# Sparse attention and a gated feed-forward block on one core: the same work under another static table of order and engines

## The chip, the cores and the metric

One core of one Trainium2 chip. The metric is the device time of one launch in microseconds, a median over runs. The engines are PE (TensorE, with its weight loads as PEld), DVE (VectorE), ACT (ScalarE), POOL (GpSimd) and SP (SyncE, which here only issues transfers). All of them work through their own instruction lists in order.

## What is computed

```python
scores = scale * np.matmul(q, k.transpose(0, 1, 3, 2))    # 8 x 8 heads, 576 x 576, depth 64
mask_local = (rel >= 0) & (rel < 32)                       # heads 0 to 3
mask_strided = (rel >= 0) & (pos[None] % 32 == pos[:, None] % 32)   # heads 4 to 7
attn = softmax(np.where(masks, scores, -1e9))
x = np.matmul(attn, v)                                     # to 4608 tokens x 512
xn = x / rms(x) * rms_g
out = (silu(xn @ w_gate) * (xn @ w_val)) @ w_out           # 512 -> 1536 -> 512
```

All in float32; the three weights come as 64-bit-wide arrays and are made into float32 on the chip.

## The kernel before, in words

**Products.** [...] Each product is then three PE products: high by high, weight low by high, high by low. A group of three on 512 columns is called a *triple* here; it is one planned operation (lines 565, 641, 1194, 1417; line 1618 has two of them). The gate and value products of chunks 0 to 2 are plain; those of the later chunks, and the output products of all but chunk 0, go in pairs of chunks by a scheme that saves one in eight products of half size (Strassen's).

**Attention.** The 64 heads are done two at a time: 32 visits. For visit n there are the scores Sn (line 291: 72 or 80 small matmuls into the bank pair, each counted as one record of 64 columns), the softmax (mask L311, maximum L314, ten exponentials on ACT L318, reciprocal L322 and L323, scaling L325, transposition L327), the values Vn (line 303) and the evacuation into a buffer raw (L361 on ACT or L363 on DVE). S0 to S4 and V0 to V3 come first and make chunk 0 of the tokens (512 of 4608); the rest is spread among the products of the feed-forward block. Visits 5 to 7 have their values in two halves.

**Chunk 0.** Each of its four quarters of x is made into xh and xl (L528 or L532, L539), squared (L400 on POOL, L403 on ACT) and summed over the partitions by PE (L408). DVE makes the root from the sums (from L485), PE spreads it (L496, the *spread*), ACT copies it (L499) and DVE multiplies the first gate products by it (L575). g(u) and v(u) stand for the gate and value products of 128 columns of the weights, each of four triples, one for each quarter of x.

**Weights.** For each block SP fetches 512 KB (L1746, names wg, wv, or), ACT makes two steps (L1761, L1766), DVE two (L1771, L1776), ACT the high part (L1781), and DVE or POOL the low part (L1783); SP writes most of them back to memory for later use (L1787, L1790). A load of q or k (L265, 288 KB) needs the slot that earlier scores read, a load of v (L275, 384 KB) the slot that earlier values read.

**Warm-ups.** Two products of ones by zeros into the bank v (L230) have no reader; they stand first on PE.

**Order.** No operation is issued as it is planned. Each is entered in a list with what it reads and writes; the constant ORDER, compressed, then gives the whole list in another sequence and for each operation the engine that takes it (many can be done by DVE or POOL, others by ACT or DVE). Within an engine the sequence is the order of its instructions. Dependencies become semaphore waits; nothing else holds an engine back, except that its instructions must have been fetched: PE's code comes in pieces of its own through the same 16 DMA engines as the data.

```python
        code = zlib.decompress(base64.b85decode(ORDER))
        left, out = list(range(n)), []
        for k in range(n):
            i = left.pop(code[k] + 256 * code[n + k])
            out.append(self.ops[i][0][ENGINES[code[2 * n + k]]][2])
        return out
```

Of the kernel before, what the change touches and what calls it, by code (L numbers as in the profile page):

```python
# [56 lines left out]

ENGINES = ("PE", "DVE", "ACT", "Pool", "SP")
ORDER = (
    "c-rk)*^^zxdGD{gPxsmPyYJiFduQJ?qir-|MrZ>hKp+VaMjMih%pyn>NyeC+f)oJ<0|5hN8yo@U;8X=WB#z@aen{mZ52?Jze?VSbsr&)y(|yjJG0%BP)ttFA_e`JeZ~c"  # L60
# [3 lines left out]
    "2%1g2wh&UYh(tTz{|o+;eUxddBtMdiuhtu6xaWwb+VZF2pZCdG3Yy)T_^WufFoYD~m6^wCKHXs`6sB@Vs~Ro>S%T+@R06*RJ2?N7wcrS$XQol`GM;+v?ZW{`l%4KYD8K"
    "l`B!<`kw9+{^Mcp$|IAH=C)5<+V$}A!{>LN>)!v(%V(+`|KifJe!g{voQY=U9=zh6dVJPfyf0Y)W-vc>Y463Ucu#O9+Iz>;>V-@DiVv(e&jp1u!>D&G9}Ox;kGEQtdyY"
    "+Z8^>x#@2aCF1cz_y)(;gAm-jdKSNFquxMQF5tHP>QDD5d&I}1DK^V{dD%{Vu;yIh;C<(6~RiaD&t{dl2OrW2)b*eVW&gX&n(ndwe<bNPv4J~s&CX~&5>PB(heZ9fq{{"
    "&*{Nzts*K)v#6xz0%q0nQHKzpnRiHDg^iCPnPn<pb#C)htcKY_P`E{yBE)v!ufp#&z}k7x!Aci8jnhDvFy8EvE{k$zOuXK7RjpT1iM|wbGMJ{jhD9#8Vg`~vsG`p;`N;"
    "!<E8Oo*($Z?dL_FxRV-ezD?{7Pjg8$A+uf+(w)P7_jrLlz;Rar<x@x;+ce!LY%k^TZTB?-FPNC@7`C)$dAU|QpWAVMs{zCJv_FV2rJm09#PBm@UcB*UD1Lv#zs;gtBCA"
    "75~J4-v9qEoOc1v_UKV(Uz9VA<y%WL99VnT|`0V|Hkk1JgJ2p4oNH_CC|JEz=CxZo^%f<&JLi<we~b8b*KG2&W9O5bA@5Zue}jrCF^KYuwOTt#Xy+b^2rsG>o630U=$#"
    "L&iMPv`O72(<YfTCWtj8Cq;Gl?`2~l30vKe_S(ch&>pMTYBldjwd#GlS~)}y&XO52P1Z<>jPD^G(r=UVwAmpIjm(p(cvz`SHKxe;1R=u#>65`2VZHSpS?;i%VYHo)`pR"  # L70
    "s5M&x6ColKGn*#m>!U;^}@``<9r{yj|nMw^7ja1z5fhC!tcJ?D!t=yaQ(wJQy1)XOy}PgP(s_b(6+R`VM4!tVGA{Mm3<=e5Bi{m%vPUYzR<nz%pqAB~&ijh}QUdw9G#b"
    "a5Y`Rfcj2suzouH_CrMSuR(gR4VqMaH>=KVt5mF41g|OWzk*T5<E5cc!fSXgD>aT>wYf(=ee?9_D}n}iaQT1`iljBzV+>xOgB6T8o?f@joDQ=-^rIDZx$f7at}g$Du@C"
    "IrcQ{&z_Fo!7wdZrtgfxKtcyTR!vo#XcVlKU&=!tqSc~TlJsVFs6O++_;kcs@Rs!q~EzCM?XPN1(CGOf)yuiXU6Ksezo#IM|1f`%}4Ct--X8z8`tv*z|;_gbmO7=Ga+Z"
    "R_BcrYJ_md<@+ezH96OyjUofFRcjT34HvW(H=BA2z@_pi|Ba7J%j-^8oLm?C#m+kM6V~T!h;KjIho)S=9zw=X|Tv(^r~aXWJs-bIx&K6`RZ<6OS8ssKZ~6?dQRl``~l0"
    "o4?t}vwGh<#d?CV;r-w3E^5|0Lg|ub&c9*c*L73pZipz;Ug)@*)7EVC56FgV2K~jH0XhtL#6y$!B8Lr4OE-+0bwmGgGt_xb*FNy`?*X&5z}9^&%(<=>IGSVstD`&o-za"
    ";Qg(hK|RwmRY_Rq<e)C?cd1I8{8&2esyopChXA||2aBrocmAQndq=K`Fg2Xi#S<Tcy3iTkWYY9=v?*Gu*dqn;;E5rTgaYB&$%a{R?31Vza5!L-1zEU4aJgdahnDDqj2H"
    "TYf#Z^QwK-xT%qI&q2rqT~EkNUR?5tY?UUv4stWHO>ez5dxiGd{e)`UvJZM;51CY@R|Xjy>cHtsZqc>2Eg<>J&dlRf5r$9N0$&mUlIEp`Vw6L<2*-aJ%+G-lU7miF+vO"
    ">jhdVyqQ67mCZcyEz848q1W^sa5>9r2_=k&|2?V<a+kq`1WM8Lv$|To4f+x^n`_V(@l_KpKYpvBLvhP_T=*-U3cmY*jpA)hQh2rGjtrsvFFcS`H1iW4ZxE<gDc&HZaE-"
    "#t>lE1AqE4EHPG~*g?<n+d1s?ezS{d{=D-`>!xO~HUQYep|2o;Uf9!c3npa~>=hA@cO8hY;^~#x+ATPWVT(yjMYWw|ba|i=|so%Z_L4>9HJ}sIuIGxvkHN0gKqwLdd+j"
    ">+?0&CF`yB{2z6-*_Fq9%UkYRv|gdc#YJj9T+r!ciTAAuJD-m&-oBkMQuE!Gqpz32=cbE{$Ux@yvxqw|w}YWsYhkH^4D3%9g~vLJY-VB8#YWj~QmaVsna?9*CjUH(bo3"  # L80
    "1FGd#6_(#EJ@0g87$7TXnA4mtR!a?V4)#ivEw1tU0G-_}Hh;U@18y^?2TPPLfkv|Fi2j^X)B9^Pp>DB!xu9m6(gPUkx3U0{qjHWk<~fER3^yAd``xa`{G2@4=E00XBnE"
    "dWdsEZ}5tXo$Dt4lxtP)hURx2GfCKk75lI{Cy_QaG;t-Ii<Yc6BamR&=LT(#qU+q;zZX-UZ@0*xdM;`&bnaPV46bONw7h)Oij}`*EHME-~iS1HNK`%&7@T0z}jSqX~f`"
    "^Q4ksdMErmPP*<oDR&nYwQA<EQE_CoG0El=XtOaw9&j!~FgFoGK_4Zg491V|fe%L$QjLz{3Vtia(JF{v-@xlB~Fjqd*9N77fx<R+?=ks`$b*70R9+<_vPp}QUI+Q^(r;"
    "%F3CLt(65rFj^R`0TE9|biHp)z7clrN$ZDxzbE=g^6x_z?2<&F!O}wN4MLI@HjFf?I@FtBkh95q2k=JGg(FJ-d$PZ_%dLHRIq4?hkZ;=(!$j)1XD6al6}_frHSo%U4jT"
    "G%TThab;*08V`<@+S^NJeS5L8e7tzv%-vba&6v05hG=|X9PCHc-BAvOQE#ak1$DjeM^#h__o3!s(q&FA=O9}!5t;L<xa=a|nDuhYMsLYogxh%s^txy2mZOKd=`#b0+IB"
    "7yQFVzn0}N>sh+5RdHpjfyE^u1TF<RCTA$yB?5{pEH0v9fh9WM|W^O?iAW?7oXxXZz|!4`0H1H(6nt2>wz+|YEbY6v#)nK&SRLP6)ABk0V;y2!l^goqUmUY9Y)F$D-s0"
    "Z4~_=Gd&zx0o3-AvM9afUOuyEXKs1384lAQZXX}`?Q2H<==&;O)z3%VQ}r5=6OGJ!KaVH7s$*ZgbWK^K#^@AavJD6Cyu|51PfA~VZnfRX$T{F`|S}uOrO!H#pxcpYGAG"
    "*VIU$4XaU%T`O8E@GX}PFQK1Ow2*v0DqkG?p6G%ULuZ>X6LKOpD#;ZIk@D*bp$7@VK&XylSM?}hfM3G^%33{Tb;h{P3ygk(D8Yen-V@JcDJ82LQq13c#q{sD3z&paElD"
    "8KcK|81g)o%o~5-iRDpxkV2`tniJHF1o6J+~I(Mu0utUeQmiT6)vkg(@hXqcc`GA6rwF=#j=P<Ay_hMqN$EyXL80oiR)L(v&erG*R99L`4tuzD|32hr~9kSY=`s%)A&e"
    "BU`fs&v4QBL}Ro?pE9NA=_RTb2{X5@t!wMry0)&ZYwOy&wyyv07i@)K>)N`uuKyc0!Gx0J0swJ?l3PkBrQ#zo1&YNBgV-hRL9F0pCHWBx;sGEmzg_|?K5vQ@D)-9mn5M"  # L90
    "@e*^;c2<eB^<woo8g3PB{<hmr$ASfU~kBy}Sx5+z@NA+c3FBFV@5M1G=Jya-n6ki6SiS1-JIfuwhIbVMo`Jr&xMf9R(3G`&krOZF3WoQyPoO(DrdD@jTdN$wE-+AH-i*"
    "?=<-WEfM)QadOEGC}f<$RkNSWOUMBVIcXs=PJ}>v)W9XG%^c6lEQ$bCM3a^?#m}KH_2|YVYw6!N`y#>IswwK)YU8**`Z9L@<^<vo5T-EoskcTT9iJi93`TOvLw|bPi7`"
    "00>x>n#E$j~u~Y#g*+Q^1GzD0q5Q%6d;FZ>j%~D`y2vzx$qH$_v<{i!~$TZ35A^BxXvQAU@66F^j`IDeoW-xOIh>97>oJc_@UswfSnUHCh9*crR$q|_(>6WsBDBDM|B$"
    "@D3#V9E>!ve*dvqDleD07%*fB{tr3adofN?;V7R02u?lQ4&pAlFC|NU9<Y8zrjjkX0w|1oR{~5VTQ6$pVrUhag2UR_T#$66uNDtpY<--X)?^IAHm27CP7z;EboFKnxpj"
    "OfX1sx+_Uh7F2nwXhwkwsfejcBq@CnB|R}$g_B4;NN**hAyqU~WpD$-Nt_dt6oyoEQou_Nl#0{JO@WQm$D4VJWQ)RtWM2xv%@jmaE|dg7Q&y3g%$PS#CQUK2ndwpsh%!"
    "kyO-As;lH;*LM~0@fM*iTQX0GFGQ5Itw6Por9EHkZ?5~UiGj7?~o7E#T316N79Wgyj`B$u-KB~=n7LLo#l4VIj?(VCK{BrzZfahiKcJc@fIzYxVVQk(LCq*%a;N+_iHO"
    "?fhTmJ~(emnt(=LR7U+8SoUB((1(N6ppfODq2!d$MPsn3Q8HSfGy9FL^a8}w2F!Bm!L>V;uEVvB9cZ(x`U((AP*|-*%_4zmG87XvnG_arIh2cPLWkwiX5u^qpB8Exe=6"
    "31j>J`T6<bdIE8<5lNNc_Qxp<2Wio!FdP;$*sxj?QIO`xd?Tu*}%M#mE^2&mA9-vCr2>6?Dn>r<F38Rf-g0vN=>X+{rZS)SD8l{*w?ao-COO+fRDV6~y3h2qZ#F)(3$k"
    "DVgA#Im(J>gN6>oh=#k7`^)3T<f(OBu2iq7ks90=bgf0(4UhA=|H{Wwn+nPDi#BmM{uzqDP?zA;ntRNjlmn#>|wPQ-Z>ZtBH&U%Al4yO0#K@$P^Mqb}0$S4w603fSHYj"
# [1825 lines left out]
```

## Time and profile before

| | |
|---|---|
| median of 3 runs | 925.74 us (924.26 to 926.48) |
| profiled execution | 925.52 us, span 923.5 us |
| PE, PEld, DVE, ACT, POOL busy | 98%, 80%, 80%, 51%, 27% |
| PE matmuls | 8722 |
| instruction queue of PE's code (q8) | 69 packets, 1.13 MB |
| data moved | 220.78 MB, mean 239 GB/s |

Times in rows are microseconds from the start of the span. A row of a timeline merges neighbours of one form: start, length, engine, line, operation, tiles, count, and in brackets the idle time before it with what ended it. "issue" in a chain or a bracket is time in which the engine waited for nothing that the profile shows. [...]

### The profile page before, as it was taken

What the parts mean: (1) busy time and instruction counts of PE and PEld (TensorE: products, weight loads), DVE (VectorE), ACT (ScalarE), POOL (GpSimd) and SP (SyncE); (2) the same over time, 40 slices, a digit from 0 to 9 for tenths busy, and PEclk for the clock granted to TensorE, in tenths of its full rate; (3) what the DMA queues carried; (4) which work ended last, traced back from release to release, by engine and by line L of the source; (5) the groups of instructions that cost most, each with busy time, mean ns of one, the idle gap of its engine ahead of it and who ended that gap; (6) DMA issues with size and microseconds to landing.
All of it is one profiled execution on the core that took longest, in us unless ns stands there. A gap on an engine that the chain in (4) does not pass through costs nothing.

```text
span 923.5 us, 21815 instructions
## 1 busy us (share of the span) xinstructions
PE 903.0 (98%) x8722; PEld 735.0 (80%) x8722; DVE 739.2 (80%) x1219; ACT 469.4 (51%) x1324; POOL 249.8 (27%) x216
## 2 busy tenths in 40 slices
...
GB/s 314 261 348 257 173 337 235 253 276 299 151 219 193 309 255 295 380 126 246 296 190 166 233 244 362 291 161 238 191 167 184 243 337 221 178 229 250 184 169 103
DMA packets 95093, 220.78 MB, mean 239 GB/s; under 512 B 9616, under 2 KB 28688, under 8 KB 94992
## 3 DMA queue, kind: packets, MB, share of 16 engines
...
q8 instruction: 69, 1.13, 0.5%
...
HBM read 172.17 MB, written 47.19 MB: 238 GB/s over the span
## 4 chain that ended last, share of the span: by engine, by line
PE 96%; DMA 1%; issue 1%; DVE 1%; ACT 0%; SPq 0%; DVEq 0%
PE acc L1618 11%; PE acc L1417 8%; PE acc L565 8%; PE v L1618 7%; PE g L1618 7%; PE v L565 7%; PE g L565 7%; PE v L1417 5%; PE g L1417 5%; PE acc L641 4%; PE g L1029 4%; PE v L1029 4%; PE acc L1029 4%; PE pair L291 3%; PE pair L303 3%; PE v L1194 2%
## 5 line engine op out<-in xcount | busy, mean ns | idle before, releaser
L565 PE MATMUL g<-xh,wg 128*128 128x512 f32 x184 | 59.3, 404 | 0.0
L565 PE MATMUL v<-xh,wv 128*128 128x512 f32 x184 | 58.3, 398 | 0.0
L318 ACT ACTIVATE pp<-pp,mx 128x64 f32<-128x64 f32 x160 | 53.3, 339 | 6.7 <-DVE mx L314 6.7
L318 ACT ACTIVATE pT<-pT,mx 128x64 f32<-128x64 f32 x160 | 53.4, 340 | 6.3 <-DVE mx L314 6.2
L696 POOL TENSOR_TENSOR tt<-tt 128x256 f32<-128x256 f32 (+1 forms) x32 | 27.5, 866 | 71.0 <-DVE tt L696 49.7
L291 PEld LDWEIGHTS pair<-xx,xx 64*32 64x32 f32 (+1 forms) x2432 | 27.8, 109 | 22.1 <-issue 14.8
L291 PE MATMUL pair<-xx,xx 64*32 64x64 f32 (+1 forms) x2432 | 33.9, 234 | 10.3 <-issue 5.3
L565 PEld LDWEIGHTS g<-xh,wg 128*128 128x128 f32 x184 | 34.9, 194 | 7.4 <-issue 0.2
L565 PEld LDWEIGHTS v<-xh,wv 128*128 128x128 f32 x184 | 33.5, 188 | 7.2 <-issue 0.2
L565 PE MATMUL g<-xl,wg 128*128 128x512 f32 x92 | 36.7, 399 | 0.0
L361 ACT COPY raw<-pair 128x160 f32<-128x160 f32 (+8 forms) x61 | 20.2, 376 | 31.3 <-PE pair L303 31.2
L565 PE MATMUL v<-xl,wv 128*128 128x512 f32 x92 | 35.9, 390 | 0.0
L565 PE MATMUL acc<-xh,wg 128*128 128x512 f32 x104 | 34.2, 411 | 0.0
L565 PE MATMUL acc<-xh,wv 128*128 128x512 f32 x104 | 33.0, 398 | 0.0
L1636 ACT ACTIVATE or<-g 128x512 f32<-128x512 f32 x24 | 14.3, 597 | 33.2 <-PE g L1618 32.2
L318 ACT ACTIVATION_READ_ACCUMULATOR pT<-pT,mx 128x1 f32 x160 | 30.9, 193 | 0.0
L318 ACT ACTIVATION_READ_ACCUMULATOR pp<-pp,mx 128x1 f32 x160 | 30.7, 192 | 0.0
L641 PE MATMUL acc<-or,hh 128*128 128x512 f32 x96 | 30.0, 394 | 0.0
L1618 PE MATMUL acc<-wg,wv 128*128 128x512 f32 x102 | 28.6, 389 | 0.0
L1618 PE MATMUL acc<-wv,wv 128*128 128x512 f32 x102 | 28.6, 389 | 0.0
L303 PEld LDWEIGHTS pair<-pT,vt 32*64 32x64 f32 x784 | 17.9, 136 | 9.1 <-issue 5.6
L303 PEld LDWEIGHTS pair<-pp,vt 32*64 32x64 f32 x744 | 17.8, 140 | 8.4 <-issue 4.0
...
## 6 DMA issues: line engine op xcount, KB each, us to landing
wv<-wsv SPq DMA_DIRECT2D x36, 512.0 KB, 7.0
wg<-wsg SPq DMA_DIRECT2D x26, 512.0 KB, 6.8
or<-tg SPq DMA_DIRECT2D x22, 512.0 KB, 5.8
tl<-tg SPq DMA_DIRECT2D x21, 512.0 KB, 5.7
th<-tg SPq DMA_DIRECT2D x21, 512.0 KB, 5.0
...
```

Of the source, the lines that this page charges most:

```text
L291: nc.tensor.matmul(out=pair_[32 * y:32 * y + m, h, 64 * g:64 * g + 64], lhsT=q[r, PAD + a:PAD + a + m], rhs=k[r, a:a + 64], start=True, st ...
L303: nc.tensor.matmul(out=dst[z // 2][64 * h:64 * h + 64, z % 2, 320 + c:320 + f], lhsT=v[r, 6 * h + j], rhs=t[r, a:a + f - c], start=j == fi ...
L318: nc.scalar.activation(out=tv[:, g], in_=tv[:, g], func=AF.Exp, bias=m[:, g:g + 1], accum_out=z[:, g:g + 1])
L361: nc.scalar.copy(out=d, in_=s)
L565: nc.tensor.matmul(out=out, lhsT=wt[:, w, sl], rhs=xhl[x, kc], start=(n == 0 and i == 0), stop=(n == KC - 1 and i == 2))
L641: nc.tensor.matmul(out=acc[t], lhsT=x[h][:, sl], rhs=wt[:, w], start=(u == 0 and i == 0), stop=(u == NU - 1 and i == 2))
L696: elementwise(width, lambda e: both(e).tensor_tensor(out=dst(), in0=a(), in1=b(), op=ALU.subtract), [], keys)
L1029: nc.tensor.matmul(out=banks[bk], lhsT=w, rhs=X[a, k].tile(y), start=start and k == 0 and i == 0, stop=stop and k == 1 and i == 2, skip_gr ...
L1194: nc.tensor.matmul(out=banks[bks[j]], lhsT=tile(v, k, j), rhs=x.tile(y), start=start and k == 0 and i == 0, stop=stop and k == KT - 1 and ...
L1417: nc.tensor.matmul(out=banks[bks[j]], lhsT=w.tile(v, k, j), rhs=x.tile(k, y), start=start and n == 0 and i == 0, stop=stop and n == KT - 1 ...
L1618: nc.tensor.matmul(out=banks[bk], lhsT=w, rhs=xtile(a, k, y), start=start and k == 0 and i == 0, stop=stop and k == 1 and i == 2, skip_gro ...
L1636: op("ACT", act(CH, True), 0, lambda: nc.scalar.activation(out=temp(dst), in_=banks[bk], func=AF.Copy, scale=scale), reads=bank_keys(bk), ...
```

## The change

ORDER is replaced by another string of the same kind. Nothing else differs.

```diff
 ORDER = (
-    "c-rk)*^^zxdGD{gPxsmPyYJiFduQJ?qir-|MrZ>hKp+VaMjMih%pyn>NyeC+f)oJ<0|5hN8yo@U;8X=WB#z@aen{mZ52?Jze?VSbsr&)y(|yjJG0%BP)ttFA_e`JeZ~c"
...
+    "c-rk)>2DlIcCWL$y87<vnd!MX!y)J3DP9sqij*koB4sO<WZ60_TV7d$WJ^BfICktvmhH8T^?G*=U$L`}HnBH=fn6jUY>dq!n|un84*`Mz`2+GLL6Scr)m7C)+TR1@18b"
...
 )
```

Both strings decode to the same 3614 operations. 349 of them go to another engine: 108 from POOL to DVE, 103 from DVE to POOL, 69 from ACT to DVE, 67 from DVE to ACT, and one each between ACT and POOL. On PE 788 of 1007 operations change their place, by up to 25; on SP 531 of 570, by up to 103.

The start of PE's list (W a warm-up, sq a sum of squares over the partitions, g0.1 the triple of the gate's block 0 with quarter 1 of x):

```
before  W W S0 S1 S2 V0 S3 V1 sq S4 g0.0 V2 g1.0 g1.2 v0.0 V3 sq sq g1.1 sq
        g0.2 g0.1 g1.3 g0.3 v0.2 spread v0.1 v1.0 v0.3 v1.2 v1.1 v1.3 g2.0 g2.2 g2.1 g2.3 V4
after   S0 S1 S2 W V0 W S3 V1 sq S4 g0.0 V2 v0.0 g1.0 g1.2 g0.2 V3 sq sq sq
        v0.2 v0.1 g0.1 g0.3 g1.1 spread g1.3 v1.0 v1.2 v0.3 v1.1 v1.3 g2.0 g2.2 g2.1 g2.3 V4
```

The start of SP's list (xx with the slot that a q or k load fills; one k load is ACT's; cb, gt and id are small constants):

```
before  xx0 cb wv0 xx3 xx2 gt xx4 xx0 wg0 wg1 xx3 vt0 xx2 xx1 vt1 wg3 wg2 or2 wv1 xx1 xx4
        vt1 vt0 id wv2 or0 vt0 wv4 wv3 wg9 wv10
after   xx0 cb wv0 xx2 xx3 wg0 xx0 xx4 wg1 xx2 vt0 gt xx1 or2 wg2 vt1 wg3 xx3 xx4 xx1 wv2
        vt0 vt1 wv1 or1 id or0 vt0 wv3 wg7 wv6
```

DVE's operations between the mask of S3 and the mask of S4 (m maximum, r reciprocal, a and b the two weight steps, lo a low part, T a transposition, * the scaling):

```
before  r2 m3 lo(wg0) *2 a(wg1) xh0 b(wg1) xl2 a(wg2) onesr xl0 T2
after   m3 r2 *2 a(wg1) xl0 b(wg1) a(wg2) a(wg3) T2
```

Between the scores S7 and the first half of V7 PE has eleven triples before and twelve after.

## Rows read from the trace of the kernel before

**Rows 1.** The page, parts 1 and 4: busy time, and the chain by engine.
```profile
PE 903.0 (98%) x8722; PEld 735.0 (80%) x8722; DVE 739.2 (80%) x1219; ACT 469.4 (51%) x1324; POOL 249.8 (27%) x216
...
PE 96%; DMA 1%; issue 1%; DVE 1%; ACT 0%; SPq 0%; DVEq 0%
```

**Rows 2.** Busy time by stretch: length, engines, PEclk, DMA share, GB/s.
```profile
57.90:135.00 77.10, 76.98 (x790) 62.57 (x791) 74.17 (x120) 67.97 (x165) 27.47 (x21) 1.00 0.75 263
...
138.00:920.00 782.00, 781.92 (x7074) 638.38 (x7072) 619.02 (x1011) 357.23 (x1009) 210.04 (x169) 1.00 0.68 232
```

**Rows 3.** The same view of the first 60 us; the third number from the right is PEclk.
```profile
7.80:38.50 30.70, 18.50 (x580) 14.63 (x580) 23.95 (x48) 27.38 (x107) 6.93 (x6) 0.50 0.84 284
38.50:42.00 3.50, 3.50 (x100) 3.14 (x99) 2.70 (x6) 2.39 (x9) 0.00 (x0) 0.99 0.92 301
42.00:48.80 6.80, 6.80 (x22) 5.65 (x21) 5.28 (x18) 5.28 (x15) 2.73 (x2) 0.50 1.02 411
48.80:60.00 11.20, 10.98 (x136) 9.04 (x135) 9.75 (x16) 8.74 (x25) 1.69 (x2) 1.00 0.99 406
```

**Rows 4.** Timeline of PE, 0 to 26 us.
```profile
1.49 3.42 PE L230 MATMUL v<-e,ones 128*128 128x512 f32 x4 [1.49 <-DVE ones L212]
5.02 0.96 PE L291 MATMUL pair<-xx,xx 64*32 64x64 f32 x72
9.33 1.38 PE L291 MATMUL pair<-xx,xx 64*32 64x64 f32 x80 [3.35 <-DMA xx<-in_qT_dram]
...
16.92 0.32 PE L303 MATMUL pair<-pp,vt 32*64 32x32 f32 x2 [1.40 <-DMA vt<-in_vl_dram]
```

**Rows 5.** The chain that ended last, 0 to 60 us: start, length, what.
```profile
19.85 3.05 issue
...
26.28 0.36 issue
...
33.31 0.43 issue
...
34.87 3.99 PE acc L565 x9
...
39.87 1.88 PE v L408 x16
...
42.92 1.50 PE v L408 x8
...
47.19 1.28 PE acc L565 x3
...
49.38 0.69 PE acc L565 x3
```

**Rows 6.** DMA queues from 13.8 to 20.4 us: packets, MB, share.
```profile
q1 hardware_dynamic: 813, 2.28, 96.5%
```

**Rows 7.** DMA queues from 20.4 to 21.6 us.
```profile
q8 instruction: 1, 0.02, 4.9%
```

**Rows 8.** DMA issues from 12.7 to 13.8 us: KB, us to landing.
```profile
wg<-in_wgv_dram SPq DMA_DIRECT2D x1, 512.0 KB, 7.4
```

**Rows 9.** Timelines of DVE and ACT, 23 to 32 us.
```profile
23.89 0.82 DVE L311 SCALAR_TENSOR_TENSOR pT<-pair,cb 128x640 f32<-128x640 f32 x1 [2.97 <-PE pair L291]
...
28.72 0.75 DVE L539 SCALAR_TENSOR_TENSOR xl<-raw,few,xh 128x512 fp32r<-128x512 f32 x1
...
31.50 0.78 DVE L311 SCALAR_TENSOR_TENSOR pp<-pair,cb 128x640 f32<-128x640 f32 x1
...
28.59 1.43 ACT L1766 ACTIVATE wg<-wg,few 128x512 uint32<-128x512 uint8 x2
```

**Rows 10.** Timelines of PE and DVE at the hole near 136 us.
```profile
136.60 0.78 PE L303 MATMUL pair<-pT,vt 32*64 32x64 f32 x40 [1.11 <-issue]
...
133.67 1.95 DVE L325 TENSOR_TENSOR pT<-pT,mx 128x640 f32<-128x640 f32 x1
...
55.78 0.82 DVE L325 TENSOR_TENSOR pp<-pp,mx 128x640 f32<-128x640 f32 x1
```

More of the change, by code (lines that the diff above doesn't have):

```diff
@@ L59 @@
 ORDER = (
-    "c-rk)*^^zxdGD{gPxsmPyYJiFduQJ?qir-|MrZ>hKp+VaMjMih%pyn>NyeC+f)oJ<0|5hN8yo@U;8X=WB#z@aen{mZ52?Jze?VSbsr&)y(|yjJG0%BP)ttFA_e`JeZ~c"
-    "A0@4MG7YemcUERP`9Hw~NWgrDV(ZSlwot&=yb6W6Ri@vd48*KndJe9W-Fb;P*Mxcl@W;~R!;ho_DEEW<l)MxId$?zHbV^4<gXZ5MJzWb%Wvkuh_0-~Hho>n8H`RsMUI<"
-    "MsG<P22lFQK<3e^?Eq}U;aQFF8!{;C(HhvS7zmlV}+sXRNId8?{2=&Lc0-0_AiT`{gpqK`}KV9Z|XlU)Y^7w|Ih43G51fO);{~`&0p4X?5j`y_LCv|?T^`S`ak@2nf>a"
-    "c-i;4GxY7Ic{iU0|=;M0l^B)yI|7qvR_D?=7uKwl6tDhA0AAY=&pD2Bp4?md8{e}N-pdb6-BdzNF;Jx6zVe{Si?Z&$+Z@s-T@z&Uz`uF|tJ1@@t>1#fZU-@4DWgOw%&%"
@@ L64 @@
[L64 to L99, printed above, removed]
@@ L100 @@
-    "1n_8t`a12V=*oaBc_-_?Sj`+*bv>NXRaV`q`e-(Wjk={A;AlEvW%<V&^B_*0&F0aR;75%)Lv!jiqG@TUmb#fclNoyhda~bS1CJtSk_`i!-IV#3aHA<JC~)I6yJ;*`d^6"
-    "4&VMhT&rd|<R%0nm}I2BM*Nor?`oos9ZHN!}zQ;rKnq(qjzGH40qau-VLATtUQ^r#w8vxGveaD^zpl#@zjHePLjGQ*}qQaW~GWmI+|bxr;fyn%MWifYqZA8jLP)-r-Zq"
-    "rrO9m^zws(MCcP+D9KpHh@Vtm^33Q^|1^#jSVA!(LV&^rco}FBza4Ie+24_q;$+k1WVC$^r28n#Pojw{14k;"
+    "c-rk)>2DlIcCWL$y87<vnd!MX!y)J3DP9sqij*koB4sO<WZ60_TV7d$WJ^BfICktvmhH8T^?G*=U$L`}HnBH=fn6jUY>dq!n|un84*`Mz`2+GLL6Scr)m7C)+TR1@18b"
@@ new lines @@
+    "TyJze!)z4z+(e(!OdvX?kP7+~Pjz@^m0modh~#{7bvv%{C|hh75wMekODyQX6XSJ^|Hxf`Z=>~i!7z7%r9LhczxPa|Sc+p);;h~GEIH-jVQX<~T98C#n=i^xWQ<@C{&l"
+    "O9>d|Knh5e`LM--#83baBZ<|PX9;KTd3lHZ<CpSZS-2ci%OT<79O>8LwU=N+93wqa!vNznEj@f`&H|&THkC;wpb-D{$-sNewX{I^4qV!{Hl^ezy4Y2ukXF~59kZ@cWv|"
+    "YzYSXGn@^jcRz6-B`m+!HpEdlSMzt?LkG}l*jj=E9RiB)__tV8MqTZj-KMp&e{b=qZ`q3)++<`xy9(F(ZsPfT=mGKW^AN^>Ye?0cy``zMuq5J+jcKvPNdD~lh!+CxD&O"
+    "77pzU}NTy>-j!8LxNmyySjRc7Obb-S_P$e&`IJt>v1}zm>cDAiw(zK7TvB!TBq9gI#ye+-}}J``T;hVe1vxiVAmz+}Cd9Uu4g}a3EmM9`)JHl|xTGxpMuv$DilVJbP&0"
@@ new lines @@
+    ")9W{HtR24j<l(2*Tz>6pbaiiZmG518{A~E>6uo$*bJcD<k>6YZXL|gF>dbTJPEPQLrzg+w{bN_dlap&F)-E{{k2#wcedk!;dHig@2Oi9I+MUJRLz55XMoyo0t&_uz+=="
+    "?o?}f$tH|xiXo8{w2hgOdkLAiEtEh)8DR}Un~YGUszE(c9}ac!tF->4Lp>oq$Ms^dI2+bSoG>Cw`ZlT1YYR?q1cW;(k%)1|^>Azzry&-BYq*X<^qTQ4LdBe|rAno-_s#"
+    "9_6X`(FF;+NH1>l^!WaUg8D$Gx=6<s_;ziW<HAc1jj4k=0-GE&WGXj#ll=6-Z-0!_XYjfjiLi(zw9UCb+}yI?I$7jRva(C<hhG(wA-BuqxwueoUVn{iSBsSt$MrN@@UH"
+    "&X?s({P0vaCZoXT{$0Ha0q#ytndi9{ysx^DH;h<JsbQ_fgr?z*_acjHgU1!-TJL4rMNyeN`F+Vcu=G}HY;^vwSzZtoX>mPHxBi>=paq~?#Zmh(Y>hWs43Y<Mb=md*_vo"
@@ new lines @@
+    "Pa3_LS{>Z>s1z{UO&rU$-NBxbfh5C#W?_f$g92^AGqV{)x69*_-}B`<QPZ*?-Tm*KOZxC(DV&oxS`gc5k;Gb>{5R&~6JMJG7U2;iAKL^P&0jaD$h4BjLq*@w#0oEb_wW"
+    "5})UMHYeU5<3arqUYp|+WzNU?j@>&k(kUE9`TofF^VSfXYc?7SjrnOd^#@bz@QagE3v6PNjjyoj`Vuo2p|Q@5<=9+p&FpKPT{ae`jk!}sbEq)}CTWj$={~waY5NFeyJ_"
+    "p-e2YE5uSs_`===dPd2M!n-;FE#zzm+aG=ax2;wjw6UEKfAUJrN1@fhx#J@EvOb^_ACxK&-L;_BxWTrE%F(m#&P{{08@xc^`F%(z(fo37b?Cy&rbyMwx~j}DL0*6=XCw"
+    "+dhvfaYTJnfgaV3-v~Qw(+|LxLODHB`{MigS)?IfQfoi8w0~t0P+vy3Amq5<u}(S!9)X(9fWm1^p+}K@q+Jp3x(Tj-}m5=*oD;yj+KG``-PDrcjNfUp-TKznLAPUa<LO"
@@ new lines @@
+    "#;bA)j<53Pw_dwA*bssqCZ;be$<+z3G4Tsvm**HY(1At)@;;6zf0eG%(WEO*|F@yJb*FI(}@s4GUyyy%&%ex(Bqgu_IoFbQu>DfNNVD$L7LDBhYTtQ`{<>DZ4%KrXR&0"
+    "nTPe#Ax2Jh2ySz<)5~aR-CSIcpNKumeX;s~el{ad^u?jfP(}P>!xA0CGV0QV1h>J|ytrWz%(H6Gs>Xn+WtbuzR3u!qK+Tew_H=jp61zHfs(nqZu1b6d~-6u}+Plj`_<d"
+    "TsH&a{{?|y`Ohzg_~!@gq=?HLd}^URjG+%EO=LLJ%rFfW8UKVSy_+N8^{}xgw5I~dp>->7dCytn=$8!Se3P5*aQkbQTfFvF=}S;gSeaG6U?wBQqDg@hIzOSr{};~;|IK"
+    "uO0jMo>07OheunPz%qQ8L_g1-XS>CJ19!mlx~ZDb%+Ck8<P<6(&M=z$m^P$0p^dm8~h8v6jbZwG<rzxjrUWDVJfmpMW)GBNsf0Da(zn)nN`H)<j8vY19S3!Od7%65Y4r"
@@ new lines @@
+    "%Z}IBjwyDgqA`Q#3YG*;su0|s7)3f=z5k3(DNap&jj?Q`KjSphQWPH*iJZw7+nDDP5K5kAT>^tQzilkyoPOjKeUb`$V~9uAwbujzIoFDPXL6L;1vch8yI{&gfKv705I`"
+    "A@~0Ho0DT6aX~H8%OardF7OheM#Vi4UBXAp<1VT}w0eBgL-qMnIOaXv1FJHUOcR^s7;8~&LQFiq3;llup7)|4JlLG)|A1z-jTNlcuGDxP;ggFLYKVrlFC|!yUK^Q|6tu"
+    ";{yb08|)Gm9ad`lLBu;M|L%p4YcI^b5Y-Dz{uK0c^c?v@+Y+e>7M>{8BJo3-(XWuK<6RU1PwUnFog9_y#DQb{xuW(^?V7IolSzP?)z2;;imEWR_OLl3k(Gys&3(HZk(_"
+    "Ejl@GM&l+9NY4n3KgyLxat0Y%2^;wZ+vOO>(+Gywt7E0&733y4l<Sm+Nh^UMLZnU{R3hBoxQ`!-`Py=x?+3U>fPsL$P)8hB@DxB}CbVeYHM%*cMeU$Qs|UC@%a`yj2fi"
@@ new lines @@
+    "5>aPH0~$GcudC~xLU-dbX=KIaO=wX6S(DiJ{fj=LDd99cevrbjBI+H)!nCnjr})Pl57G@+4$I1Kk=%f(*Kby?u}&XnabX2l{E1a0^jdlYl=VhqRF!+8Uv70jLr&?35qT"
+    "pkId#c6{gF({|RV%7))7`liUsYlQN7{o^rSY;9jWDi`nF+>6|WEQ+j1ru@863{asq+;Hp2qqBG5+bpkLkK}6@&|elavNG!x<UY!(+5m;g1Yw^ly10|1qn2Ssx(7{8Uqo"
+    "C=jKvflMrH&p@!Je^pPvRI2ba>5@x#4F<h|_6VZ19wnzBDu>j^I1LHJJa6)d9cAbH1?$g3v2CrJ?!Gq?0zG}kV7eeElzhpso*QYbkv~Bv$_z<yrkoAd);iOo;(rht<z!"
+    "4HK0W?(V;gJuE`GV7o@fBe%!*$$(HPnW<RkBXO0?VC@bBip@=h$K73v%;4a}^oDplk&KVl3}9mVq@#8*`fr^r+zRqmvapv5pTN#JvP}@NyULUOr9R!;ACn`LQ;_urqmM"
@@ new lines @@
+    "qJw~6zuvF=U0AJDyfQ2e!EWPRrvYb*6}td<JXtuw*N=hWs8w#ax@BuLH!=i@thp4jny>-5<E2;t%rQq3vv?&igK7;}6*o*k-zfmk!?8<<yTOc#<C=uh0u+3>zv}Fx!-C"
+    "F+kd=cG3K5FX7{Fa8fGyX9&WK@|NsXC?L6Ur-V4C@**o3}?aSUB1mh*tQg0XDdAOT?rJIHoyn&T071){|jvLs*_&j=!*0_Ly?Ng<CI5*C`VEsn%YrD8#ER?21pHyc6)D"
+    "+?$PPoN5p@(4oDhtvsZNCU*kC&WO|7P<`AFn)k+NZ1_#B|(<r?bTOU2fmm$k%=g>Jwmt@TGkaocP4`Q^wgWirE`x#f%1n<eCCvKy7Vp<<%b$Yx_O5S8iWuDskJrYynw1"
+    "AQD0sZSf@CJ7Bz%PxL<t&U%qTWboY|j5j}E_LvPd?5oHd3>^ZOi%Xz$F9f;WZoPF?26fwTa@xDEn9bYh}8nbws)}|)xYTsF<of@u^;8g=M>cBI0)u>O`PqxNyAbLNl^y"
```

14 lines of the change are left out of this document (added).

## The prediction

> **What bounds the kernel now.** I read the page first. TensorE is busy for 903.0 of 923.5 us, and the chain that ended last is 96% PE [rows 1]. A busy matmul row can hide waiting, so the second view was the table by stretch: from 57.9 us to 135 PE is busy 76.98 of 77.10 us, and from 138 to 920 it is busy 781.92 of 782.00, at full clock [rows 2]. A triple (three 512-column products) takes 0.69 us there [rows 5]. Behind 58 us the same products cost the same in any order, so a new order can gain only before 58 us and in one hole near 136 us, and can lose anywhere. The third view was the granted clock of the first 60 us: half from 7.8 to 38.5, full to 42.0, half again to 48.8, full from there on [rows 3]. The fourth was PE's start row by row [rows 4], and the fifth the chain of the first 60 us [rows 5]. The reader is to see three things in them: a stop of 3.05 us inside the scores S3 that nothing but "issue" ended, a run of triples from 34.87 us at half clock, and a second such run from 44.4 us, each behind small work.
>
> The profiled execution took 925.52 us (span 923.5, 2.0 around it), 0.22 below the median 925.74. A difference of 0.2% (1.85 us) is about what a measurement of this kernel can tell from none.
>
> **The change part by part.** The decoded table holds the same 3614 operations, so no product is added or removed and PE's sum stays. What moves:
>
> *Warm-ups.* Both leave the front. They took 3.42 us there, but the scores S0 began at 5.02 us, right behind them and about when their inputs landed [rows 4], so S0 starts no earlier. S0 will run at half clock: 1.38 (S1's row) in place of 0.96, 0.4 us more. That is covered, since ScalarE's exponentials of S0 waited for the weight wv0 before them. One warm-up (1.7 us) now stands ahead of V0, which waited 1.40 us for its vt load [rows 4], so at most 0.3 us is added; the other stands ahead of S3, whose first rows run into the 3.05 us stop whatever happens. Taken: 0; bounds 0 and 1.1. If the stop went wholly, that cover would be gone and the second warm-up would cost its 1.7.
>
> *Code against loads.* The stop at 19.85 is a wait for code. The DMA engines moved data alone from 13.8 to 20.4 us, 2.28 MB [rows 6]. The one packet of 0.02 MB on the instruction queue came after that [rows 7], and PE went on at 22.9. The fetch of wg3, issued at 13.02, landed 7.4 us later, at 20.4 [rows 8]. So the piece moved when what had been issued by about 13.8 was through: xx3, vt0, xx2, xx1, vt1 and wg3, 2.14 MB. In the new order SP has by then issued xx2, vt0, xx1, or2 and wg2, 1.98 MB; xx3, vt1 and wg3 come behind, wv1 later still. The difference is 160 KB, at 345 GB/s (2.28 MB in 6.6 us) 0.4 us. Bounds: nothing, and the whole 3.05. I take 0.4, the nearest to what was really moved: the loads are mostly exchanged for others of their size. SP then blocks on the same kind of wait as before (a q/k load that waits for S3 to leave its slot), with xx4 now ahead of it, so that the next scores have their input.
>
> [...]
>
> *DVE and ACT from S3 to V2.* From the mask of S3 (23.89) to that of S4 (31.50) DVE does twelve operations between, 7.6 us in all [rows 9]. In the new order wg0's low part goes to POOL, xh0 comes before, xl2 (0.75) goes behind and one weight step comes in: nine between, about 6.4. What is late next is ACT: it makes two weight steps of wg2 and wg3 (28.59 to 30.0, rows 9) behind the evacuation of V1, and DVE needs them. V1 comes 0.4 to 0.8 earlier (the 0.4 above; the 0.36 stop at its end, rows 5, is the next piece of code); I take 0.7. So V2 begins 0.7 earlier, and its own stop of 0.43 goes or stays; taken: gone, since fewer bytes are in flight when that piece is asked for. The triples behind V2 then begin at 34.87 - 0.7 - 0.4 = 33.8. Bounds 0 and -2.
>
> *Triples, V3, sums.* Before, three triples stand between V2 and V3 and one between the second and third sum; now four stand before V3 and the three sums are together. Four triples at half clock: 3.99 + 1.28 = 5.27, V3 at 39.05. V3 takes 1.0 (38.87 to 39.87), two sums 1.88, the third 1.50 (its square is ready by 41.8, since ACT needs some 1.75 from V3's end): 43.4, against 42.92 + 1.50 = 44.4. Gain 1.0.
>
> *Five triples to the spread.* Both orders have five here. Before they took from 44.4 to 50.07, 5.65 us. Before the clock rose at 38.5 PE had run triples from 34.87, and before it rose at 48.8 from 44.4 [rows 3, 5]. If it rises as far into the run from 43.4 (4.05 us, the middle of the two), that part at 1.28 holds 3.2 triples and the other 1.8 take 0.69 each: 5.3 us, spread at 48.7. Gain 1.2 us in all. Bounds: 0 (as slow as before and the earlier terms lost) and 3.4 (full clock kept throughout, 43.4 + 3.4 less the half us that the third sum gives).
>
> *Behind the spread* DVE's nine operations to the end of the next softmax stand in the same order, and PE's next ten triples with them, so V4 near 58 us comes 1.2 earlier as well. ACT and DVE are almost full up to 100 us, but they gained the same time, since both stood idle in the 3.05 us.
>
> *The hole at 136 us.* V7's first half waited 1.11 us for its softmax, one step of which took 1.95 us on DVE, where the same step took 0.82 at 55.8 us [rows 10]. Between the scores S7 and V7 stood eleven triples, now twelve: 0.7 off the hole. Bounds 0 and 1.1.
>
> *The rest.* 788 of PE's 1007 operations change place, 349 operations change engine (DVE and POOL exchange 103 for 108, ACT and DVE 69 for 67). PE switches between triples and small work 67 times in both. SP's loads move by up to 103 places: one reload of weights near 755 us now has three triples less between the release of its slot and its use. Cost taken: 0, since the producers' sums are the same; what hides them is the spare time of a triple or less that most results have here. Bounds 0 and +2; if that cover is gone in one place, 0.3 to 1 us.
>
> Sum: -1.2 - 0.7 = -1.9: 925.52 - 1.9 = **923.6 us**, 0.23% under the median.
>
> **The rivals.**
> 1. *The piece of code does not follow the loads.* Then the stop keeps its 3.05 us and V2 its 0.43. Triples begin at 34.87, four make 40.1, V3 41.1, two sums 43.0, the third 44.5, spread near 49.9: nothing gained but the 0.7 at 136 us: 924.8, no measurable change. For it: how little the bytes ahead change. Against: rows 6 and 7, where the piece came behind 6.6 us of pure data.
> [...]
> 2. *The clock comes late: slower.* It rose at 38.5, 0.4 us ahead of V3 [rows 3, 5]. In the new order V3 begins at 39.05 by my sum; if the rise misses it, V3 and two sums take double (1.28 against 0.69 is the ratio), 2.9 us more, and the run of five triples starts at 46.3: spread near 51.8, 1.9 late. With the 0.7 of the hole, 926.7; if the clock falls once more ahead of the ten triples behind the spread, another 1.9: 928.6. It decides where V3 begins before the rise. For it: the three sums stand together, small work of some 4 us with V3. Against: the run ahead of V3 grows by a triple.
> 3. *A new hole behind 58 us.* An order this tight has one place where a load or a softmax comes a triple too late; three such holes of 0.7 give back the gain: 925.7. For it: the 1.11 at 136 us is one in the old order. Against: it is the only one in 860 us.
> 4. *The change does not do what it says*: the engines change too, so it is more than an order. That is in the sum.
>
> **How the numbers follow.** Forecast, faster: 0.46, its own range 921.5 to 923.9 (the clock's bound and part of the full stop). Rivals 1 and 3, within 0.2%: 0.33 together. Rival 2 with the worse end of 3, slower: 0.21. The range 920.6 to 927.9 reaches to the full-clock bound (-3.4, the hole wholly gone, a further half us of the stop) and to rival 2 without its last end.
>
> **What would show it.** Right: "issue" inside S3 shorter than 3.05; V2 before 32; the last sum before 44; the spread's matmuls near 48.7; the granted clock at full from 47 or so; V7's wait under half; no idle PE from 58 on. Wrong: the stop unchanged, the clock's last rise at 49 or later, or PE idle behind 58 us.

## The result and the profile after

The changed kernel takes **930.44 us** in the median (928.83 to 932.66, six runs) against 925.64 (924.26 to 926.81, six runs) of the kernel before: a ratio of 1.0053, 95% interval 1.0038 to 1.0069. (Here and below the ratio is the one recorded over all runs of the two kernels that were timed side by side; it need not be the quotient of the two medians.) It is slower by 4.9 us. The forecast was 923.6, with 920.6 to 927.9: wrong in sign, and the measured time lies outside the range. The profiled execution has a span of 928.6 us, against 923.5.

First the page, parts 1 and 4, against [rows 1]:

```profile
PE 904.2 (97%) x8722; PEld 732.4 (79%) x8722; DVE 751.8 (81%) x1222; ACT 470.1 (51%) x1326; POOL 244.1 (26%) x211
...
PE 79%; DVE 13%; DMA 3%; issue 2%; ACT 2%; SPq 0%; DVEq 0%
```

PE's sum has hardly moved (903.0 to 904.2). DVE's has grown by 12.6 us, from 739.2, with three rows more. DVE has 13% of the chain that ended last; before it had 1%.

Then the table by stretch, against [rows 2] (length, then busy time of PE, PEld, DVE, ACT, POOL, then PEclk, the granted share of PE's full clock, then DMA share, GB/s):

```profile
58.00:135.00 77.00, 75.48 (x695) 59.45 (x694) 74.17 (x118) 61.76 (x153) 20.12 (x15) 1.00 0.74 250
...
138.00:920.00 782.00, 778.67 (x7079) 634.35 (x7071) 629.80 (x1011) 361.86 (x1017) 208.59 (x165) 1.00 0.67 232
```

PE is idle for 1.52 us from 58 to 135 and for 3.33 us from 138 to 920; before it was 0.12 and 0.08. The waits of PE from 58 to 915 us (engine, line, what ended the wait: us in all, times, longest) name the engine:

```profile
PE pair L303 <- issue: 1.2, 1, 1.2
PE acc L565 <- DVE or L609: 1.0, 1, 1.0
PE g L565 <- DVE e L580: 1.0, 2, 0.5
PE g L1618 <- DVE or L1668: 0.8, 1, 0.8
PE g L1417 <- DVE or L1649: 0.5, 1, 0.5
PE v L1417 <- DVE e L1649: 0.4, 1, 0.4
PE v L1417 <- DVE xl L1333: 0.3, 1, 0.3
PE v L565 <- DVE wv L1783: 0.3, 1, 0.3
PE acc L641 <- DVE hl L632: 0.2, 1, 0.2
```

Eight of the nine lines end with DVE; the first is V7, which waits for its softmax and so for DVE too. With three of under 0.2 us there are 13 such waits; from matmul start to matmul start each costs 0.2 to 1.3 us, 7.9 in all. The kernel before has one of that size, V7's 1.11 [rows 10].

The start of the kernel went the other way. PE's timeline (start, length, what; [rows 4, 5] have the old one):

```profile
14.38 2.07 PE L230 MATMUL v<-e,ones 128*128 128x512 f32 x2
...
18.36 2.08 PE L230 MATMUL v<-e,ones 128*128 128x512 f32 x2
...
23.45 0.94 PE L291 MATMUL pair<-xx,xx 64*32 64x64 f32 x49 [2.40 <-issue]
...
34.13 1.22 PE L565 MATMUL acc<-xh,wv 128*128 128x512 f32 x2
...
37.35 0.63 PE L565 MATMUL g<-xh,wg 128*128 128x512 f32 x2
...
47.09 1.05 PE L496 MATMUL acc<-pT,few 128*128 128x128 f32 x8
```

The first two triples pass at half clock; by 37.35 two products take 0.63 us, not 1.22. The spread starts at 47.09 (before 49.91) and V4 at 55.19 (before 58.02): **a lead of 2.8 us at V4**. From V4 to the end of the span it is 873.4 us; before it was 923.5 - 58.0 = 865.5. So in these two profiles the new order is 2.8 us ahead at V4 and loses 7.9 behind it, of which the waits account for 6.8 (7.9 - 1.1).

**What stands ahead of a wait.** One of the 13, PE's first product g at 73.97 us, in the changed kernel's timeline of POOL, DVE and PE:

```profile
71.14 1.63 POOL L1783 TENSOR_TENSOR wv<-tt,wv 128x512 fp32r<-128x512 f32 x1 [8.01 <-ACT wv L1781]
...
71.64 1.68 DVE L1776 SCALAR_TENSOR_TENSOR tt<-wg 128x512 uint32<-128x512 uint32 x1
...
73.24 0.67 DVE L580 SCALAR_TENSOR_TENSOR e<-e,g 128x512 f32<-128x512 f32 x1
...
73.97 0.50 PE L565 MATMUL g<-xh,wg 128*128 128x512 f32 x1 [0.49 <-DVE e L580]
```

The weight step L1776 takes 1.68 us. In the kernel before the same group of twelve (tiles tt<-wg; durations in ns: least, median, most) never takes over 0.70:

```profile
L1776 DVE SCALAR_TENSOR_TENSOR tt<-wg x12: 670/684/694, 19.5 to 131.5; 128x512 uint32<-128x512 uint32 x12
```

It began 0.50 us after a POOL operation and ended 0.55 us after that one's end (71.14 + 1.63 = 72.77; 71.64 + 1.68 = 73.32): as if it stood still while POOL worked. The wait at 203.44 us shows the same:

```profile
199.75 1.75 POOL L692 TENSOR_TENSOR tt<-wv 128x512 f32<-128x512 f32 x1
...
200.28 1.77 DVE L692 TENSOR_TENSOR tt<-wg 128x512 f32<-128x512 f32 x1
...
202.74 0.64 DVE L609 SCALAR_TENSOR_TENSOR or<-hl,acc 128x512 f32<-128x512 f32 x1
...
203.44 0.73 PE L565 MATMUL acc<-xh,wv 128*128 128x512 f32 x2 [1.01 <-DVE or L609]
```

I call such a pair a *meeting*: a DVE row over 0.3 us longer than the lower quartile of the rows of its line, with a POOL row beside it. The kernel before has 35, which cost DVE 26.6 us, among them the step L325 of 1.95 us in [rows 10], beside a POOL square (L424, which adds two squares) of 133.65 to 134.94 us. The changed kernel has 49, which cost 35.8. In both, every DVE row as late as that has a POOL row beside it that began first. Ahead of each of the 13 waits a lengthened DVE row stands in the same run of DVE work, with no break of over 0.1 us between them. Such a run can be long, since DVE is almost full up to 135 us: the row ahead of the wait at 68.65 us began at 61.95. That the meetings make the waits is therefore not shown by their places alone; the experiments test it.

The text ahead of the prediction says that nothing but semaphore waits and missing code holds an engine back. These rows point to a third thing: DVE operations that began while POOL worked took 1.68 us (median of their group 0.684) and 1.95 us (0.82 elsewhere) here.

In the two pairs of rows above POOL began first, L1776 and L692 each read two tiles in SBUF by the kernel's code, and each ended 0.55 us after POOL (73.32 against 72.77, 202.05 against 201.50). By what POOL holds DVE the rows do not show.

### The profile page after: what moved, and what is told of

Its sections match the earlier page's. It is cut to its first block, busy times and chain, and to the rows that moved or that the text cites. A ratio compares the mean times of both kernels' runs of the same rounds, so it can differ in the third digit from the quotient of the medians.

```text
span 928.6 us, 21800 instructions
## 1 busy us (share of the span) xinstructions
PE 904.2 (97%) x8722; PEld 732.4 (79%) x8722; DVE 751.8 (81%) x1222; ACT 470.1 (51%) x1326; POOL 244.1 (26%) x211
## 3 DMA queue, kind: packets, MB, share of 16 engines
q8 instruction: 69, 1.13, 0.5%
## 4 chain that ended last, share of the span: by engine, by line
PE 79%; DVE 13%; DMA 3%; issue 2%; ACT 2%; SPq 0%; DVEq 0%
PE acc L1618 10%; PE g L1618 7%; PE v L1618 7%; PE acc L565 6%; PE acc L1417 5%; PE v L565 5%; PE g L565 5%; PE v L1417 4%; PE g L1029 4%; PE v L1029 4%; PE acc L1029 3%; PE g L1417 3%; PE pair L291 2%; PE pair L303 2%; PE g L1194 2%
## 5 line engine op out<-in xcount | busy, mean ns | idle before, releaser
L696 POOL TENSOR_TENSOR tt<-tt 128x256 f32<-128x256 f32 (+1 forms) x23 | 17.9, 787 | 54.7 <-DVE tt L696 36.5
L578 ACT ACTIVATE e<-g 128x512 f32<-128x512 f32 x23 | 13.9, 602 | 22.4 <-PE g L565 18.0
```

Source lines behind the costliest of these rows:

```text
L696: elementwise(width, lambda e: both(e).tensor_tensor(out=dst(), in0=a(), in1=b(), op=ALU.subtract), [], keys)
```

## The experiments

All change ORDER alone; diffs are of its decoded form. Theory S says that DVE operations which meet POOL operations, ahead of what PE waits for, make the loss; L that the lead could not be kept anyway; Q that DVE's new sequence puts work in the wrong place and POOL has no part. The old kernel was timed again beside each group of runs; the changed kernel was not, so its 1.0053 comes from other rounds than the ratios set against it.

**Front and body.** The two orders are cut at V4.

```diff
-ORDER = old
+ORDER = new up to V4, then what is left of old in old's sequence and on old's engines
```

> The changed kernel's order and engines up to V4, the old kernel's order and engines for all that comes after. In the profiles V4 begins at 55.19 us in the changed kernel and at 58.02 in the old one, a lead of 2.8 us; behind it the changed kernel loses 7.7 us more than the old one. Theory S (the loss is the new body's own: DVE operations that run beside a POOL operation take about 1 us longer, and they stand ahead of what PE waits for): the lead of 2.8 stays, 925.6 - 2.8 = 922.8 us. Rival L (the lead cannot be kept, because DVE or the loads set the pace up to 137 us): V7 begins at 136.6 as before, 925.6 us. Rival Q (the new DVE order alone puts work ahead of what PE needs; POOL plays no part): 922.8 too.

Measured: 924.50 us (12 runs) against 927.13 of the old kernel (29 runs), ratio 0.9982 (0.9964 to 1.0000): 1.7 us less. V4 at 53.93, 867.5 us from there on. V7, which L wanted at 136.6 as before, comes 4.1 us earlier:

```profile
132.46 0.92 PE L303 MATMUL pair<-pT,vt 32*64 32x64 f32 x40 [1.11 <-issue]
```

Behind it some 1.5 us are lost again, at operations that now come late (0.76 of it at a reload at 718.8 us).

```diff
-ORDER = old
+ORDER = old up to V4, then what is left of new in new's sequence and on new's engines
```

> The counterpart: the old kernel's order and engines up to V4, the changed kernel's for the rest. Theory S: the waits behind V4 are the body's own, so they stay and the lead is missing: 930.4 + 2.8 = 933.2 us. Rival L: the changed kernel lost its lead anyway, so without it the end is the same, 930.4. Rival Q: as S, 933.2.

Measured: 934.46 us, ratio 1.0075 (1.0052 to 1.0099): 6.9 us more. From V4 to the end 875.1 us, with twelve of the changed kernel's 13 waits at the same operations and 50 meetings. The new body costs 6.9 us behind the old front, and (1.0053 - 0.9982) x 926 = 6.6 behind the new one. The lead is 1.7 us with the old body and (1.0075 - 1.0053) x 926 = 2.0 with the new. Both are at the edge of what the intervals can tell, so the times alone do not settle L; V7's place in the first run speaks against it.

**POOL's part.** Thirteen POOL operations of the changed kernel, 19.6 us of POOL, go to DVE (four low parts L1783, one L632, one L424, and seven sums and differences planned at line 686: three of L1333, one each of L692, L786, L933, L1392), each ahead of the operation that it lengthened:

```diff
 DVE:
+  low part of a weight block L1783 (before on POOL)
   weight step L1776 of 61.95 us
...
```

> The changed kernel with 13 POOL operations moved to DVE, each placed directly ahead of the DVE operation that ran beside it and took about 1 us too long. Nothing else moves. Theory S: each costs DVE some 0.7 us and gives back some 0.8 to 1.1, so the 13 waits of PE behind 58 us shrink by up to 0.4 each: 927 to 929 us, and at least not slower than 930.4. Rival Q: DVE is the late engine and gets 13 operations more of 0.4 to 0.8 us, most of them straight ahead of what PE waits for: some 6 to 8 us more, 936 to 938.

Measured: 926.26 us (12 runs), ratio 0.9993 (0.9979 to 1.0008), against 1.0053 of the changed kernel: 5.6 us less, more than S gave. The page:

```profile
PE 901.4 (98%) x8722; PEld 731.7 (79%) x8722; DVE 749.2 (81%) x1235; ACT 469.3 (51%) x1326; POOL 223.5 (24%) x198
```

DVE has 13 rows more and 2.6 us *less* to do than in the changed kernel (751.8). There are 36 meetings left. Q falls: it wanted 6 to 8 us more. Not all is won back: from V4 to the end it takes 869.3 us, against 873.4 and, in the kernel before, 865.5, and five waits of PE are left, 3.0 us in all.

**One meeting in the kernel before.**

```diff
-POOL square L424 (at 133.65 us)
 DVE  softmax L325, L327 of visit 7
+DVE  square L424
```

> The old kernel with one operation moved: the square of 1.29 us that POOL makes at 133.65 us goes to DVE, behind the softmax that V7 waits for. In the old profile the softmax step L325 beside it took 1.95 us, and 0.82 elsewhere. Theory S: L325 takes 0.82, V7 no longer waits, its 1.11 us are gone: 925.6 - 1.1 = 924.5. Rival Q: L325 keeps its 1.95 us for another reason, V7 waits as before: 925.6.

Measured: 926.52 us, ratio 0.9995 (0.9982 to 1.0008). POOL in the kernel before ([rows 10] have its L325 and V7):

```profile
133.65 1.29 POOL L424 TENSOR_TENSOR ssq<-ssq,srt 128x512 f32<-128x512 f32 x1 [3.61 <-ACT srt L419]
```

DVE and PE around V7 in this run:

```profile
135.31 0.83 DVE L325 TENSOR_TENSOR pT<-pT,mx 128x640 f32<-128x640 f32 x1
...
136.94 0.65 DVE L424 TENSOR_TENSOR ssq<-ssq,srt 128x512 f32<-128x512 f32 x1
...
137.12 0.91 PE L303 MATMUL pair<-pT,vt 32*64 32x64 f32 x40
```

L325 takes 0.83 and V7 waits for nothing. From V4 to V7 it is 137.12 - 59.65 = 77.47 us, against 136.60 - 58.02 = 78.58: the 1.11 us, to the hundredth. The whole time shows only half of it, and its interval holds zero as well: the local gain is shown, a gain of the kernel is not. One thing that takes it back is a load for which PE did not wait before and now waits 0.5 us, at 722.6 us.

**A version that beats both.** New front, old body, the square of the run before, and three operations that the profile of the first run showed late (the reload goes two places earlier in SP's list, not one):

```diff
-POOL square L424
+DVE  square L424, behind the softmax of visit 7
...
+SP   reload that PE waited for at 718.8 us
 SP   two reloads that wait for triples
-SP   reload that PE waited for at 718.8 us
...
+DVE  gate L580 of 231 us, L1649 of 386 us
 DVE  a high part and two low parts; a split and a sum
-DVE  gate L580 of 231 us, L1649 of 386 us
```

> The kernel with the new front and the old body, with four operations moved that its profile shows late: the POOL square that ran beside the softmax step L325 at 129.5 us goes to DVE behind that softmax (PE waited 1.18 us); the reload that PE waited for at 718.8 us (0.76) goes one load earlier on SP; two DVE gates that PE waited for at 231 us (0.47) and 386 us (0.26) go ahead of the DVE operations before them. Theory S: with the new front 2.8 us and with the waits up to 2.7 more: 3 to 5 us less than the old kernel, a ratio of 0.995 to 0.997. Rival: each removed wait shows up again at the next late operation, and it stays where new front and old body alone are, 1.7 us under the old kernel (0.998).

Measured: **922.94 us** (11 runs) against 925.98 (32 runs), ratio 0.9956 (0.9940 to 0.9973). PE by stretch:

```profile
57.90:135.00 77.10, 77.10 (x774) 62.34 (x767) 73.69 (x120) 67.65 (x164) 25.54 (x17) 1.00 0.72 257
138.00:910.00 772.00, 772.00 (x6996) 631.05 (x6997) 619.37 (x1007) 356.80 (x1006) 210.30 (x169) 1.00 0.68 233
```

No idle time is left there. The interval leaves out the rival's 0.998. In this profile V4 begins at 57.46, though the front is the new one: what is won ahead of V4 varies from execution to execution (below).

**The warm-ups.**

```diff
-PE: warm-up, warm-up, S0, S1, S2, V0, S3
+PE: S0, S1, S2, warm-up, V0, warm-up, S3
```

> The old kernel with nothing but the two warm-ups moved: one ahead of V0, one ahead of the scores S3, as in the changed kernel. If the warm-ups' place makes the lead (they fill the stop at 19.85 us and lift the clock earlier): V4 near 55 us and 922 to 923 us. If they only fill time that was idle anyway, as the prediction had it (cost and gain 0): V4 at 58, 925.6, no change.

Measured: 926.33 us (ten runs), ratio 1.0006 (0.9990 to 1.0022), V4 at 57.44: no gain.

```diff
-PE: S0, S1, S2, warm-up, V0, warm-up, S3
+PE: warm-up, warm-up, S0, S1, S2, V0, S3
```

> The changed kernel with nothing but the two warm-ups put back to the front. If their place makes the lead: it is lost, V4 near 58 us, 930.4 + 2.8 = 933.2 us. If the triples ahead of V3 and the three sums together make it: V4 near 55.2, 930.4.

Measured: 932.42 us, ratio 1.0066 (1.0044 to 1.0088), where the changed kernel has 1.0053: 1.2 us more, with intervals that overlap. V4 at 57.79 in this one profile. The old kernel shows no gain from the warm-ups' new place; whether a part of the new front's lead hangs on it is not settled.

**Code and loads.**

```diff
-SP: ... vt1, wg3, wg2, or2, wv1, xx1 (waits for S3), xx4 ...
+SP: ... vt1, xx1 (waits for S3), xx4, wg3, wg2, or2, wv1 ...
```

> The old kernel with the four loads wg3, wg2, or2 and wv1 (0.5 MB each) issued behind the q/k load that waits for the scores S3, so that only what was issued by 12.6 us is outstanding when PE stops at 19.85 us. If the piece of code moves behind the loads that are outstanding (as in the prediction): some 0.5 MB less, 1.5 us at 345 GB/s, and PE goes on at 21.4 or earlier, the stop under 1.5 us. Rival (the piece does not follow the loads): it moves at 20.5 as before, the stop keeps some 3 us. The late loads may cost up to 3 us between 26 and 40 us; the time itself is not what is read.

Measured: 928.59 us, ratio 1.0014 (0.9989 to 1.0039). The instruction queue from 17.9 to 19.0 us, and PE:

```profile
q8 instruction: 1, 0.02, 5.7%
```

```profile
20.35 0.94 PE L291 MATMUL pair<-xx,xx 64*32 64x64 f32 x48 [1.17 <-issue]
```

The piece moved at 17.96 us, not behind 20.4 [rows 7], with no data packet beside it up to 19.0, and the stop is 1.17 us, not 3.05 [rows 5]. With these loads held back the piece came 2.6 us earlier (17.96 against 20.52), so here it followed the loads, and the rival falls. What was won was lost again: with wg2 and wg3 late, V2 began at 35.22 in place of 32.34.

**Order or engines?** The 211 operations that changed between DVE and POOL are exchanged alone.

```diff
 sequence of the changed kernel
-its choice between DVE and POOL
+the old kernel's choice
```

> The changed kernel's order, with the 211 operations that changed between DVE and POOL put back on the engine that the old kernel had for them (the exchanges with ACT stay new). If the choice of engine makes the meetings of DVE and POOL operations: lengthened DVE operations fall from 49 to about 35 and the time by some 6 us, to 925. If the order makes them: 49 and 930.4. A third outcome: order and engines only fit each other, and either half alone is worse than both, over 932, with operations that stand too early or too late in their new queue.

Measured: 957.57 us, ratio 1.0331 (1.0314 to 1.0348), 83 meetings that cost DVE 70.5 us.

```diff
 sequence of the kernel before
-its choice between DVE and POOL
+the changed kernel's choice
```

> The counterpart: the old kernel's order with the changed kernel's choice between DVE and POOL for the same 211 operations. If the choice of engine decides: lengthened DVE operations rise from 35 to about 49, and 931 to 932 us. If the order decides: 35 and 925.6. Third outcome as in the run before: over 932 in both.

Measured: 959.74 us, ratio 1.0347 (1.0316 to 1.0379), 77 meetings, 65.1 us. DVE on the two pages:

```profile
PE 915.8 (95%) x8722; PEld 734.4 (77%) x8722; DVE 779.2 (81%) x1217; ACT 469.1 (49%) x1326; POOL 258.1 (27%) x216
```

```profile
PE 913.1 (95%) x8722; PEld 734.5 (77%) x8722; DVE 776.0 (81%) x1224; ACT 470.2 (49%) x1324; POOL 255.8 (27%) x211
```

The third outcome: sequence and engines fit each other only as pairs, and a mixture has about twice the meetings. How much of the 31 and 32 us they make is not separated: in the mixtures some waits of PE end with POOL or ACT themselves. Over all kernels, from V4 to the end:

| kernel (front / body) | meetings | cost to DVE, us | V4 at | V4 to end |
|---|---|---|---|---|
| old / old | 35 | 26.6 | 58.02 | 865.5 |
| old, square moved | 34 | 24.6 | 59.65 | 865.6 |
| old, warm-ups moved | 36 | 26.6 | 57.44 | 865.3 |
| old, loads held back | 36 | 26.5 | 59.82 | 867.1 |
| new / old | 36 | 26.3 | 53.93 | 867.5 |
| new / old, four moved | 37 | 27.3 | 57.46 | 863.8 |
| new / new, 13 to DVE | 36 | 27.2 | 54.28 | 869.3 |
| new / new | 49 | 35.8 | 55.19 | 873.4 |
| new / new, warm-ups back | 48 | 35.4 | 57.79 | 874.2 |
| old / new | 50 | 37.4 | 57.84 | 875.1 |
| old sequence, new DVE/POOL | 77 | 65.1 | 53.91 | 902.7 |
| new sequence, old DVE/POOL | 83 | 70.5 | 57.23 | 902.5 |

The number of meetings is not all: 36 go with 865.3 us from V4 to the end in one kernel and with 869.3 in another, where five waits of PE come to 3.0 us. In the version that beats both, 37 of them leave PE no idle time in the two stretches above.

## Why the prediction was wrong

**The step that failed is "The rest"**: cost 0, bounds 0 and +2, "since the producers' sums are the same; what hides them is the spare time of a triple or less". The runs put 6.6 to 6.9 us in its place: waits of PE behind DVE operations that took longer beside POOL. Both halves of the reason failed. The producers' sums are not the same: DVE's grew by 12.6 us, 9.2 of it (35.8 - 26.6) in meetings, because the new sequence and the exchange of 103 for 108 operations change what runs beside what. And the spare time of a triple, 0.69 us, did not cover a step that took 1.0 to 1.1 us longer (L1776 with 1.68, L325 with 1.95) where DVE worked almost without a break, as it does up to 135 us (74.17 of 77.10 before). A row that showed it was quoted: L325 with 1.95 against 0.82 [rows 10]. I took it as a size of the hole and did not ask what stood beside it.

**Rival 3** (new holes behind 58 us) had the right kind: it said three of 0.7 us, and there were 13, of 0.2 to 1.3. Its "against", that the old order has one such hole in 860 us, was no evidence on the new one.

**The hole at 136 us**: -0.7 was wrong. V7 waited 1.25 us; the same square on POOL lay beside the softmax again (L325 took 1.62). One triple more ahead of V7 did not help, because DVE was late from the start: a low part L632 took 1.78 us beside a POOL operation, and the mask of S7 began 2.44 us behind the start of the scores, before 1.13.

**Warm-ups**: taken 0, and 0 it was with the old body (1.0006). S0 began at 4.99 and took 1.33, close to what was worked out; each warm-up took 2.07 or 2.08, not 1.7.

**Code against loads**: with the loads held back the piece moved at 17.96 us and the stop was 1.17 us, as the mechanism has it. The size, -0.4, is not shown: the piece moved at 21.10 us and PE went on at 23.45, 0.55 later than before. One load more seems to have stood ahead of it: vt1, issued at 14.26 and landed 6.6 us later, which the prediction counted as coming behind. The stop is shorter (2.40) because S3 began later, behind the second warm-up. Rival 1 falls as a mechanism; its forecast for this place, nothing gained, was nearer than the -0.4.

**DVE and ACT from S3 to V2**: -0.7 was wrong, V2 began 0.19 later (32.53); that its own stop of 0.43 would go was right.

**Triples, V3, sums, spread**: predicted spread at 48.7, measured 47.09 in this profile. The triples began at 34.13 (predicted 33.8), but the clock was at its full level before 37.35 and not at 38.5, so V3 began at 38.13 (predicted 39.05) and the sums with it. The second stretch at half clock was about 3 us long (43.5 to 46.5, rows below) and not 6.8 [rows 3]; the sum had it falling into the run of five triples as before. That the spread came earlier than forecast is owed to this and was not foreseen. Rival 2, the late clock, did not come about. The lead in the timed runs, 1.7 to 2.0 us, has the predicted 1.2 inside its interval. The profiles with the new front and the warm-ups inside have V4 at 53.93, 54.28, 55.19 and 57.46, those with the old front and its loads at 57.84, 58.02 and 59.65. But the old sequence with the new choice between DVE and POOL, warm-ups at the front, has it at 53.91. (Two operations of that front go to POOL in place of DVE; whether they have a part in it is not shown.) And with the new front and the warm-ups inside, V4 is at 57.46 where the granted clock was 0.50 from 42 to 48 us (the version that beats both) and at 55.19 where it was 0.50 only from 43.5 to 46.5 (the changed kernel). So V4 moved by 2 to 4 us with the front or the sequence unchanged, as much as between the fronts, and one profile is no measure of a front.

**Signs**: "issue" in S3 under 3.05 (2.40), last sum before 44 (it ended at 42.1) and the clock at full from 47 or so came; the spread came 1.6 us before its 48.7, and V2 before 32 did not. "No idle PE from 58 on" and "V7's wait under half", which decide the time, both failed.

**Left open**: why this pair of sequence and engines has 49 meetings and the old one 35. The mixtures show that both avoid most of what a mixture has; what the maker of the table knew of meetings no trace tells. The kernel's own code gives a hint: its list of operations has a mark named port (lines 113, 130, 686, 1772, 1777), set on what POOL does and on several kinds of DVE operation.
